# Four-layer spectral and convolution network on one core: complex sums on 128 partitions, inverse steps as two accumulating 64-row products

## The chip, the core and the metric

The kernel runs on one core of a Trainium2 chip. The core has TensorE (PE in the profile; its weight loads are listed apart as PEld), VectorE (DVE), ScalarE (ACT), GpSimd (POOL), and SyncE (SP), from whose queue nearly all DMAs are issued. PE writes its products to PSUM, which has eight banks of 2 KiB per partition; DVE and ACT read them there, POOL works on SBUF tiles alone. The metric is the device time of one execution in microseconds (us). Three timed runs of the kernel before took 786.98, 787.42 and 789.71 us; their median is 787.42.

## The reference

The input x is a sequence of 2048 rows with 512 channels in fp32. Four layers are applied in the order A, B, A, B, each on the layer norm of the running x and each added back to it:

```
def _A_ref(x, w_r, w_i):            # spectral layer
    X = rfft2(x) * (w_r + 1j * w_i)
    return irfft2(X, s=(S, D))

def _B_ref(u, ...):                 # long convolution per channel
    K = 2 * einsum("dn,dnl->dl", C, exp(A * dt * l)).real
    y = irfft(rfft(u, 2L) * rfft(K, 2L), 2L)[:, :L]
    return y + u * D_skip

x = x + _A_ref(_layernorm(x), ...);  x = x + _B_ref(_layernorm(x), ...)
x = x + _A_ref(_layernorm(x), ...);  x = x + _B_ref(_layernorm(x), ...)
```

What matters here is the middle of each layer: a spectrum is multiplied by complex weights (A) or by the spectrum of the convolution kernel (B), and is then transformed back.

## The kernel before, in words

All Fourier transforms are matrix products with constant matrices, split into small steps. The network runs through these stages:

- `layer_a` for the first A layer: `spread` (norm and the first step along the sequence), `middle` (16 groups q, each with `forward`, `weigh`, `back`, one group behind the other), `end` (`fold` and `rows_back`). Beside it runs `kernel_time`, which builds the convolution kernel K in the time domain and is the longest piece of work for DVE.
- `layer_b` for the first B layer: channels come in four blocks of 128. Per block there are the products along the rows (`forward_b.rows`), DVE transposes (`turn`), four `pair` products whose results `weigh` multiplies, the inverse products `back.units` and `back.rows`, and an add to x (line 1001). Between the four blocks stand the remaining three of the four blocks of `kernel_freq`, which take the spectrum of K by the same forward steps; what is left of `kernel_time` is filled in between.
- `layer_a` again, now without other work beside it, and `layer_b` again, whose K spectra are read back from DRAM (tile kk, line 956).

The order of the work on each engine is that of the lists of steps (`interleave`, and the lists in lines 1036 to 1064), within which the Tile framework orders instructions by priority and by its own model of time when the program is built. On the chip each engine takes its instructions in that fixed order.

The complex product in `layer_b.weigh` (lines 953 to 975). A `pair` fills one PSUM tile of 128 partitions by 512 for each of the two planes (real, imaginary). Its two partition halves are two halves h of the frequencies u, and each has 64 rows of spectrum for 32 channels. DVE multiplies each plane by the real and the imaginary part of the weights (line 962), which gives four tiles `m[c, pl]`. The sums are made by halves: for each h a subtraction of 64 partitions goes to partitions 0 to 63 of Y (the real part), and an addition to partitions 64 to 127 (the imaginary part). That is four sums of 64x512 per `weigh` (line 974), 16 per block. The strings `YB = 'vgggvggg'` and `YC = 'vgggvgggvgvgvgvv'` name the engine of each: v is DVE, g is POOL. YB, used twice over, puts 4 of a block's 16 sums on DVE; YC, used in the last block of each B layer, puts 7 there.

The inverse step. `units(j, d)` (line 977) treats 8 channels. For each it multiplies the 128 rows of Y (real over imaginary) by the constant MBT, in two products that go to the two partition halves of one PSUM bank; ACT copies the bank to V (line 987). `side_by_side` (line 308) only issues products after each other; two whose outputs lie in different partition halves use different column halves of PE's array and can run beside each other. Every fp32 product is two MATMUL and two LDWEIGHTS instructions in the trace. Before the first unit of a channel half, one product with the constant MIX replaces frequency 0 (line 982), with an ACT copy back to Y (line 983). `rows` (line 990) then makes the rows of the output.

In `layer_a`, `weigh(q)` (line 518) has the same form: four sums of 64x257 per q (lines 532, 533), with engines from YA and YA2, and one small sum for an edge column (line 534). `back(q)` (line 537) has four products of 128 rows, all into one PSUM bank, and two ACT copies (line 548).

PSUM pools. A `phase` line gives banks to tags: p1 holds forward products, p2 the pairs, p3 inverse products. In the first A layer p1, p2 and p3 share five banks. In the first half of the first B layer (`PM = '2,3,0'`, up to chain step 4) p1 and p3 share two; in its second half (`PB = [5, 3]`) they share five. From the second A layer on, p3 has three of its own.

## Time and profile before

| | |
|---|---|
| median of three timed runs | 787.42 us |
| profiled execution: span, first to last instruction | 781.1 us |
| what lies around the span (difference of the two) | 6.3 us |
| instructions | 18929 |
| ACT busy | 428.1 us (55%) |
| POOL busy | 404.9 us (52%) |
| DMA moved | 80.64 MB, mean 103 GB/s |
| mean granted TensorE clock | 0.934 |

The stages, read from the places of their lines in the trace (us from the start of the span): middle of the first A layer 78 to 156, its end 156 to 240, first B layer 285 to 540, middle of the second A layer 565 to 615, its end to 662, second B layer 662 to 781.

How to read it: a "lines" row gives line, engine, operation, tiles (out<-in), shape and count, then the busy time of the group (overlaps counted once), the mean duration of one in ns, the idle time of the engine just before them, and what ended it. "128*64" behind a matmul is the part of PE's array that it uses, rows by columns. PE's instructions overlap, so that a mean duration is far longer than the time per instruction. A "windows" row gives the stretch, its length, the busy time of each engine with its count of instructions, the granted clock, the DMA share and the rate. A "timeline" row gives start, time covered, engine, line, operation, and in brackets the idle time before it and its releaser.

### The profile page before, as it was taken

The page shows a single profiled execution, that of the slowest core. Times are in us where ns is not written, and L with a number is a line of the kernel's source. Part 1 is how long each engine was busy: PE and PEld are TensorE (multiplying, and loading weights), DVE is VectorE, ACT ScalarE, POOL GpSimd, SP SyncE. Part 2 cuts the span into 40 slices and gives each one's busy share as a digit, 9 for nine tenths or more (in the row PEclk, how much of TensorE's full clock was granted, in tenths as well). Part 3 has the DMA queues.
Part 4 walks back from the last instruction along what each step waited for, and adds up shares of the span by engine and source line. Part 5 has one row for each costly group of instructions (what it writes and reads, how often), then busy time and mean ns, then how long its engine had stood idle before and what let it go on. Part 6 is the DMA issues. An engine that isn't in the chain of part 4 may idle for free. (4 is left out here: it accounts for less than half of the span.)

```text
span 781.1 us, 18929 instructions
## 1 busy us (share of the span) xinstructions
PE 627.7 (80%) x7248; PEld 443.5 (57%) x7248; DVE 649.3 (83%) x1301; ACT 428.1 (55%) x919; POOL 404.9 (52%) x596
## 2 busy tenths in 40 slices
PE   3447888897867977998889887874899896989986
PEld 2336666665534543656365656654777663566766
DVE  7998748979998999769996997878578696889992
ACT  3433778854748765887568834323756336242312
POOL 3675876764825245721657266281055572475760
PEclk9998899999979997999989999997999999799998
DMA  8300552344546503452325539422133114234513
GB/s 311 128 0 1 129 138 56 110 75 151 114 167 184 137 9 64 124 145 82 51 68 117 192 55 257 141 95 69 55 82 83 28 28 136 70 95 120 154 29 83
DMA packets 144923, 80.64 MB, mean 103 GB/s; under 512 B 78561, under 2 KB 124513, under 8 KB 143937
## 3 DMA queue, kind: packets, MB, share of 16 engines
q1 hardware_dynamic: 144576, 78.90, 36.2%
q8 instruction: 58, 0.95, 0.5%
q0 software_dynamic: 256, 0.52, 0.4%
q14 instruction: 33, 0.26, 0.1%
HBM read 54.89 MB, written 25.03 MB: 102 GB/s over the span
## 5 line engine op out<-in xcount | busy, mean ns | idle before, releaser
L974 POOL TENSOR_TENSOR u<-wb,wb 64x512 f32<-64x512 f32 x90 | 129.2, 1436 | 85.2 <-DVE wb L962 75.9
L316 PE MATMUL p<-z,mb 128*64 128x512 f32 (+2 forms) x480 | 102.0, 535 | 8.3 <-DVE wb L962 5.4
L870 PE MATMUL pv<-qp 128*64 128x128 f32 x1024 | 78.9, 295 | 11.4 <-DVE qp L859 6.9
L859 DVE TENSOR_TENSOR qp<-qp,mag 128x1024 f32<-128x1024 f32 x64 | 83.8, 1317 | 1.0
L962 DVE TENSOR_TENSOR wb<-p,kk 128x512 f32<-128x512 f32 x128 | 80.6, 674 | 4.7 <-PE p L316 4.6
L870 PEld LDWEIGHTS pv<-qp 128*64 128x64 f32 x1024 | 62.0, 147 | 38.8 <-ACT stage L878 10.2
L648 ACT COPY z<-p 128x512 f32<-128x512 f32 x96 | 51.4, 597 | 58.1 <-PE p L316 43.7
L316 PE MATMUL p<-mb,u 128*64 128x64 f32 x2048 | 72.9, 235 | 10.6 <-DVE u L974 4.5
L316 PEld LDWEIGHTS p<-mb,u 128*64 128x64 f32 x2048 | 70.7, 150 | 18.7 <-issue 11.3
L857 DVE SCALAR_TENSOR_TENSOR qp<-qp,mag 128x256 f32<-128x256 f32 x128 | 64.8, 523 | 13.6 <-ACT qp L800 13.3
L654 DVE STREAM_TRANSPOSE z<-z 128x512 f32<-128x512 f32 x96 | 58.5, 673 | 18.0 <-ACT z L648 18.0
L527 DVE TENSOR_TENSOR w<-wt,p 128x514 f32<-128x514 f32 x64 | 42.6, 686 | 33.3 <-PE p L316 18.6
L1086 POOL TENSOR_SCALAR w<-w,norms 128x128 f32<-128x128 f32 x64 | 40.5, 647 | 51.9 <-DMA w<-h 28.3
L532 POOL TENSOR_TENSOR w<-w,w 64x257 f32<-64x257 f32 x48 | 40.1, 835 | 50.3 <-DVE w L527 46.2
L456 PE MATMUL p<-w,w 128*128 128x128 f32 x128 | 32.0, 429 | 40.8 <-DVE w L449 30.8
L987 ACT COPY u<-p 128x512 f32<-128x512 f32 x64 | 37.6, 590 | 43.8 <-PE p L316 43.8
L316 PEld LDWEIGHTS p<-z,mb 128*64 128x64 f32 x480 | 34.2, 140 | 37.0 <-issue 20.2
L456 PEld LDWEIGHTS p<-w,w 128*128 128x128 f32 x128 | 27.8, 318 | 44.7 <-issue 24.8
L800 ACT ACTIVATE kf<-pk 128x512 f32<-128x512 f32 x64 | 38.9, 608 | 24.1 <-PE pk L839 23.6
L316 PE MATMUL p<-t,w 64*64 64x128 f32 x1024 | 43.3, 290 | 5.8 <-issue 2.6
L974 DVE TENSOR_TENSOR u<-wb,wb 64x512 f32<-64x512 f32 x38 | 46.9, 1234 | 0.5
L800 ACT ACTIVATE qp<-kf,half 128x512 f32<-128x512 f32 x64 | 47.2, 737 | 0.1
(200 smaller groups left out, 1495.3 us busy)
## 6 DMA issues: line engine op xcount, KB each, us to landing
wt<-in_w SPq DMA_DIRECT2D x32, 257.0 KB
kf<-kk SPq DMA_DIRECT2D x32, 256.0 KB
kk<-kf SPq DMA_DIRECT2D x32, 256.0 KB
u<-in_x SPq DMA_DIRECT2D x16, 256.0 KB
hr<-in_x SPq DMA_DIRECT2D x16, 256.0 KB
kt<-stage SPq DMA_DIRECT2D x32, 128.0 KB
h<-hr SPq DMA_DIRECT2D x16, 256.0 KB
w<-kt SPq DMA_DIRECT2D x32, 128.0 KB
```

The lines of the kernel that those rows point to most:

```text
L316: last = self.nc.tensor.matmul(out, weights, data, start=not more, stop=True, skip_group_check=True).ins
L456: nc.tensor.matmul(p[:, b], xf[:, b], t, start=True, stop=True)
L527: nc.vector.tensor_mul(m[pl], W, px[:, None, :].to_broadcast([128, 2, 257]))
L648: nc.scalar.copy(tiles["z"][:, :, :, b, m:m + 2].rearrange("p u j m r -> p (u j) (m r)"), ps[b].rearrange("p u j m r -> p (u j) (m r)"))
L654: nc.vector.transpose(tiles["zt"][:, u:u + 8].rearrange("p u j d -> p (u j d)"), tiles["z"][:, u:u + 8].rearrange("p u j b m r -> p (u j b ...
L800: last["x"] = nc.scalar.activation(*a, **k).ins
L857: nc.vector.scalar_tensor_tensor(QP[:, c, 0], QP[:, c, 1, :, ::-1], -1.0 if c else 1.0, m[:, 0], op0=ALU.mult, op1=ALU.mult)
L859: nc.vector.tensor_mul(t, t, mag[:, None, 1:3, 256 * j:256 * j + 256].to_broadcast([128, 2, 2, 256]))
L870: nc.tensor.matmul(p[64 * t:64 * t + 64, g], QP[:, c, 2, d:d + 2].rearrange("p s a -> p (s a)"), QP[:, c, 0:2, d:d + 2].rearrange("p k s b ...
L962: nc.vector.tensor_mul(split(m[c, pl], "du", [32, 16]), by_channel(p), split(k[c], "du", [32, 16]))
L974: self.added = e[0].tensor_sub(y[0:64], v[0, 0], v[1, 1]), e[1].tensor_add(y[64:128], v[0, 1], v[1, 0])
L1086: (self.nc.gpsimd if XNE[k] == "g" else self.nc.vector).tensor_scalar(t[:, k], t[:, k], scale, bias, op0=ALU.mult, op1=ALU.add)
```

## The change

The 128 partitions that the complex product works on now hold two halves j of the channels, each with the same 64 rows of spectrum, where they held two halves of the frequencies. Real and imaginary parts of Y lie beside each other in one tile instead of one over the other.

- `pair`: the two halves of a PSUM tile are 16 channels each with all 32 frequencies of the step. The product for frequency 0 (i even) is now made for both halves.
- `weigh` in B: two sums of 128x512 instead of four of 64x512. YB puts both on POOL; YC puts those of the last `weigh` (i = 3) on DVE.
- `weigh` in A: two sums of 128x257 instead of four of 64x257, all on POOL.
- `units`: each product over 128 rows becomes two over 64 rows that add up in PSUM (r = 0, 1), for each channel half j (its own bank) and each half s of the output rows. So there are twice as many products, on quarters of the array (64 rows by 64 columns), and two banks are open at a time; a step now issues 32 products for 4 channels of both halves.
- `mix`: eight products of 64 rows by 16 columns in place of one of 128 by 32, two banks and two ACT copies in place of one.
- `back` in A: eight products of 64 rows in place of four of 128, two banks in place of one.
- Y and V become one tile of 32 KiB per partition in place of two of 16; U and the rows read at the start likewise. The constants grow (mb from 512 to 768 columns).

```diff
-YA = 'ggvg'
+YA = 'gg'
-YA2 = 'gvgv'
+YA2 = 'gg'
-YB = 'vgggvggg'
-YC = 'vgggvgggvgvgvgvv'
+YB = 'gggggggg'
+YC = 'ggggggvv'
...
-    return p.rearrange("p (u d) -> p d u", d=32)
+    return p.rearrange("p (u d) -> p d u", d=16)
...
             Y = self.sb("w", [2, 257])
-            for v in range(2):
-                hs = slice(64 * v, 64 * v + 64)
-                e = [nc.vector if c == "v" else nc.gpsimd for c in ya[2 * v:2 * v + 2]]
-                e[0].tensor_sub(Y[0:64, v], m[0][hs, 0], m[1][hs, 1])
-                e[1].tensor_add(Y[64:128, v], m[1][hs, 0], m[0][hs, 1])
+            e = [adders[c] for c in ya]
+            e[0].tensor_sub(Y[:, 0], m[0][:, 0], m[1][:, 1])
+            e[1].tensor_add(Y[:, 1], m[1][:, 0], m[0][:, 1])
...
-            p = self.ps("p3", [2, 2, 128])
+            p = [self.ps("p3", [2, 128]) for v in range(2)]
+            for oe in range(2):
+                for r in range(2):
+                    for v in range(2):
+                        hs = slice(64 * v, 64 * v + 64)
+                        nc.tensor.matmul(p[v][:, oe], Y[hs, r, 128 * oe:128 * oe + 128], k["ST"][hs, int(q + v > 0), r],
+                                         start=r == 0, stop=r == 1, skip_group_check=True)
             for v in range(2):
-                st = k["ST"][:, int(q + v > 0)]
-                for oe in range(2):
-                    nc.tensor.matmul(p[:, oe, v], Y[:, v, 128 * oe:128 * oe + 128], st, start=True, stop=True,
-                                     skip_group_check=True)
-            for oe in range(2):
-                nc.scalar.copy(U[oe].rearrange("p s n q (v c) -> p v (s n) q c", v=2)[:, :, :, q],
-                               p[:, oe].rearrange("p v (n c) -> p v n c", c=4))
+                nc.scalar.copy(U[2].rearrange("p o s n q (v c) -> p v o (s n) q c", v=2)[:, v, :, :, q],
+                               p[v].rearrange("p o (n c) -> p o n c", c=4))
...
-                products = []
-                for h in (1, 0):
-                    o = p[64 * h:64 * h + 64].rearrange("p (u d) -> p u d", d=32)
-                    u = 32 * (i % 2) + 16 * h
-                    c = 1 if u == 0 else 0
-                    z = tiles["zt"][:, :, i // 2]
-                    products += [(o[:, 0], MB[:, 0, pl], z[:, 0])] * c + [(o[:, c:], MB[:, 1, pl], z[:, u + c:u + 16])]
+                u = 32 * (i % 2)
+                c = 1 if u == 0 else 0
+                o = [p[64 * j:64 * j + 64].rearrange("p (u d) -> p u d", d=16) for j in range(2)]
+                z = [tiles["zt"][:, u:u + 32, j, 16 * (i // 2):16 * (i // 2) + 16] for j in range(2)]
+                products = [(o[j][:, 0], MB[:, 0, pl], z[j][:, 0]) for j in range(2 * c)]
+                products += [(o[j][:, c:], MB[:, 1, pl], z[j][:, c:]) for j in range(2)]
...
-            for h in range(2):
-                was = self.added
-                u = 32 * (i % 2) + 16 * h
-                y = Y[:, i // 2, :, u:u + 16]
-                v = {k: t[64 * h:64 * h + 64].rearrange("p (d u) -> p d u", d=32) for k, t in m.items()}
-                e = [nc.vector if c == "v" else eng for c in adders[4 * i + 2 * h:4 * i + 2 * h + 2]]
-                self.added = e[0].tensor_sub(y[0:64], v[0, 0], v[1, 1]), e[1].tensor_add(y[64:128], v[0, 1], v[1, 0])
+            d, u = 16 * (i // 2), 32 * (i % 2)
+            y = Y[:, :, d:d + 16, u:u + 32]
+            v = {k: split(t, "du", [16, 32]) for k, t in m.items()}
+            e = [nc.vector if c == "v" else eng for c in adders[2 * i:2 * i + 2]]
+            self.added = e[0].tensor_sub(y[:, 0], v[0, 0], v[1, 1]), e[1].tensor_add(y[:, 1], v[0, 1], v[1, 0])
...
-            def units(j, d):
-                if d == 0:
-
-                    pm = self.ps("p3", [32])
-                    with self.tc.issue_after(self.paired):
-                        nc.tensor.matmul(pm, MIX, Y[:, j, :, 0], start=True, stop=True)
-                    nc.scalar.copy(Y[:, j, :, 0], pm)
-                p = self.ps("p3", [64, 8])
-                self.side_by_side([(p[64 * r:64 * r + 64, :, i], Y[:, j, d + i], MBT[:, 64 * r:64 * r + 64])
-                                   for i in range(8) for r in range(2)])
-                nc.scalar.copy(V[:, :, j, :, d:d + 8].rearrange("p n q d -> p q n d"),
-                               p.rearrange("p (q n) d -> p q n d", q=2))
+            def mix(d):
+                pm = [self.ps("p3", [2, 16]) for j in range(2)]
+                with self.tc.issue_after(self.paired):
+                    self.side_by_side([(pm[j][hs, s], MIX[hs, r, 64 * s:64 * s + 64], Y[hs, r, d:d + 16, 0], *[r] * r)
+                                       for s in range(2) for r in range(2) for j, hs in enumerate(halves)])
+                for j, hs in enumerate(halves):
+                    nc.scalar.copy(Y[hs, :, d:d + 16, 0], pm[j][hs])
+
+            def units(d):
+                if d % 16 == 0:
+                    mix(d)
+                if d % 8 == 0:
+                    banks[:] = [self.ps("p3", [64, 8]) for j in range(2)]
+                self.side_by_side([(banks[j][64 * s:64 * s + 64, :, i % 8], Y[hs, r, i], MBT[hs, r, 64 * s:64 * s + 64], *[r] * r)
+                                   for i in range(d, d + 4) for r in range(2) for j, hs in enumerate(halves) for s in range(2)])
+                if d % 8 == 4:
+                    for j in range(2):
+                        nc.scalar.copy(V[:, :, j, :, d - 4:d + 4].rearrange("p n q d -> p q n d"),
+                                       banks[j].rearrange("p (q n) d -> p q n d", q=2))
```

62 lines of the change are left out of this document (33 added, 29 removed).

## The prediction, made before the changed kernel was run

> **What bounds the kernel now.** I read the page's first part, then the busy times by stage, then the groups, then the timeline of the second B layer and of the second A layer.
>
> ```profile
> PE 627.7 (80%) x7248; PEld 443.5 (57%) x7248; DVE 649.3 (83%) x1301; ACT 428.1 (55%) x919; POOL 404.9 (52%) x596
> ```
>
> Over the span no engine is full; the stages have to be looked at singly.
>
> ```profile
> core 0: us, PE busy (x) PEld busy (x) DVE busy (x) ACT busy (x) POOL busy (x), PEclk, DMA share, GB/s
> 78.00:156.00 78.00, 67.15 (x507) 49.94 (x506) 57.76 (x82) 63.57 (x138) 56.75 (x117) 0.91 0.42 108
> 285.00:540.00 255.00, 206.02 (x3007) 139.62 (x3006) 216.66 (x394) 147.32 (x285) 130.05 (x136) 0.92 0.43 112
> 662.00:781.00 119.00, 101.80 (x1870) 74.75 (x1870) 94.56 (x144) 34.86 (x67) 62.35 (x45) 0.93 0.31 90
> ...
> 565.00:615.00 50.00, 46.66 (x355) 35.14 (x355) 40.32 (x80) 29.34 (x87) 28.53 (x74) 1.00 0.29 75
> ```
>
> First B layer (285 to 540): DVE 216.7 and PE 206.0 of 255, nearly equal, DVE ahead. Second B layer (662 to 781): PE 101.8 of 119, DVE 94.6. Middle of the second A layer (565 to 615): PE 46.7 of 50. So DVE's relief counts in full only until PE is the more loaded, which comes soon. POOL (130 and 62 us) bounds nothing.
>
> In the second B layer PE's pauses are short. Three stand before the last row product of a block and are waits for DVE's add to x, which empties the PSUM bank:
>
> ```profile
> 710.76 1.09 PE L316 MATMUL p<-u,t 128*64 128x128 f32 x16 [1.50 <-DVE za L1001]
> ...
> 737.00 1.09 PE L316 MATMUL p<-u,t 128*64 128x128 f32 x16 [1.13 <-DVE za L1001]
> ...
> 758.75 1.09 PE L316 MATMUL p<-u,t 128*64 128x128 f32 x16 [2.08 <-DVE za L1001]
> ```
>
> Together 4.7 us: there DVE, late from its sums, holds PE up.
>
> **The sums, removed and added.**
>
> ```profile
> L974 POOL TENSOR_TENSOR u<-wb,wb 64x512 f32<-64x512 f32 x90 | 129.2, 1436 | 85.2 <-DVE wb L962 75.9 <-DVE wb L964 4.0
> L974 DVE TENSOR_TENSOR u<-wb,wb 64x512 f32<-64x512 f32 x38 | 46.9, 1234 | 0.5
> L532 POOL TENSOR_TENSOR w<-w,w 64x257 f32<-64x257 f32 x48 | 40.1, 835 | 50.3 <-DVE w L527 46.2 <-ACT kf L800 1.6 <-ACT w L511 0.7
> L533 POOL TENSOR_TENSOR w<-w,w 64x257 f32<-64x257 f32 x32 | 21.4, 669 | 2.3
> L533 DVE TENSOR_TENSOR w<-w,w 64x257 f32<-64x257 f32 x32 | 18.8, 587 | 1.1
> L532 DVE TENSOR_TENSOR w<-w,w 64x257 f32<-64x257 f32 x16 | 10.3, 644 | 1.5 <-DVE w L527 0.5
> L1062 POOL TENSOR_TENSOR t<-za 128x512 f32<-128x512 f32 x8 | 11.1, 1419 | 0.1
> ```
>
> A POOL sum over 128 partitions by 512 (line 1062) takes 1419 ns, one over 64 takes 1436: the partition count is free, so halving the number of sums halves the work. In B, 90 + 38 sums become 60 on POOL and 4 on DVE. POOL: 129.2 - 60 x 1.436 = 43.0 us less. In A, POOL 80 sums and DVE 48 become 64 on POOL: 61.5 - 64 x 0.75 (mean of its two rows) = 13.5 us less on POOL and 29.1 less on DVE.
>
> ```profile
> L974 DVE TENSOR_TENSOR u<-wb,wb x38: 671/1260/1799, 292.2 to 763.2; 64x512 f32<-64x512 f32 x38
> ...
> 285.00:540.00 255.00, 22.07 (x19) 66.85 (x45) 0.92 0.43 112
> ...
> 662.00:781.00 119.00, 24.83 (x19) 62.35 (x45) 0.93 0.31 90
> ```
>
> The second and third rows are line 974 alone, DVE then POOL. Per B layer DVE loses 22.1 and 24.8 us and gets two sums back, between 0.67 us (the minimum) and 1.80 (the maximum). I take 0.67, the nearest to an undisturbed one, so 1.3 per layer: net -20.7 and -23.5. The spread is POOL's doing: DVE operations with two SBUF inputs stretch while POOL works. An example:
>
> ```profile
> 313.77 6.23 POOL L974 TENSOR_TENSOR u<-wb,wb 64x512 f32<-64x512 f32 x3 [2.96 <-DVE wb L962]
> ...
> 315.69 1.48 DVE L857 SCALAR_TENSOR_TENSOR qp<-qp,mag 128x256 f32<-128x256 f32 x1
> ...
> 320.81 0.40 DVE L857 SCALAR_TENSOR_TENSOR qp<-qp,mag 128x256 f32<-128x256 f32 x1
> ```
>
> 1.48 us beside a POOL sum, 0.40 without. With fewer POOL sums this shrinks too; I count it at nothing, since DVE's net relief is already cut off by PE below.
>
> **What it is worth.** First B layer: the larger of the two loads falls from 216.7 (DVE) to 206.0 (PE; DVE would have 196.0), so -10.7. Bounds: 0 if PE's order sets the pace anyway; -20.7 / (216.7/255) = -24.4 if the stretch shrinks with DVE alone. Second B layer: PE is the larger load already, so only the three waits go, -4.7; bounds 0 and -11.5 (PE's idle 17.2 less the 5.7 between the last matmul, in a row below, and the end of the span). A layers: below.
>
> **The inverse units.** 2048 matmuls of 128x64 become 4096 of half the rows. What a matmul costs in a stream:
>
> ```profile
> 696.61 3.95 PE L316 MATMUL p<-mb,u 128*64 128x64 f32 x128
> ...
> 478.23 2.25 PE L316 MATMUL p<-t,w 64*64 64x128 f32 x72
> ...
> 771.66 3.71 PE L316 MATMUL p<-u,t 128*64 128x128 f32 x64 [0.73 <-ACT u L987]
> ```
>
> Per instruction 30.9 ns (64 columns streamed, two tiles of the array side by side), 31.3 (128 columns, four tiles), 58.0 (128 columns, two tiles). From the third to the second, four tiles instead of two halve the price at equal columns; from the third to the first, half the columns halve it. The new units have both, 64 columns on four tiles, which gives 15.5 ns, and 4096 x 15.5 = 63 us, as 2048 x 30.9 now. But no stream of the trace runs below 31 ns; the other end of the price is 31 ns each, +63 us of PE. I take 15.5: it follows two rows that differ in one thing each, and an end of 31 would mean that two different limits lie at the same number by chance.
>
> The TensorE page of the Trainium skill ("TensorE: Matmul & The Clock Gate", Wait — 56ns, not 53.3ns?) speaks against this: starts of matmuls are never closer than about 25 ns, however few columns. No row here is under it; estimated by that figure the 4096 cost 102 us in place of 63.
>
> **Banks and copies.** A group of 8 channels now fills two banks, both closed only with the group's last products.
>
> ```profile
> 768.22 0.59 ACT L987 COPY u<-p 128x512 f32<-128x512 f32 x1 [1.34 <-PE p L316]
> 769.16 0.59 ACT L987 COPY u<-p 128x512 f32<-128x512 f32 x1 [0.35 <-PE p L316]
> ```
>
> A copy takes 0.59 us and starts by the second row 0.35 us after the one before, when PE has filled the next bank; now it is hidden under that bank's products. Afterwards the two copies come together, the second free at 0.35 + 2 x 0.59 = 1.53 us after the last product, the first at 0.94. In the first half of the first B layer p3 and p1 have two banks in all, so the next group waits up to 1.53; elsewhere it has a spare bank and waits up to 0.94. 8 groups x 1.53 + 24 x 0.94 = 35 us if nothing else lay between; 0 if pairs, forward rows and the filled-in work always do. While a group waits, everything behind it in PE's fixed order waits too, pairs and forward rows among it, and behind these DVE's multiplications. But such work also stands ahead of nearly every group in the timeline, so I take a tenth, +3. The last group has nothing behind it: its second copy adds 0.6 to the end. `mix` has one more copy:
>
> ```profile
> L983 ACT COPY u<-p 128x32 f32<-128x32 f32 x16 | 3.6, 222 | 20.7 <-PE p L982 20.7
> ```
>
> 0.2 us each, on the path only at the last one, +0.2. The 96 additional small matmuls of `pair` are 3.0 us at 31 ns, half of that two at a time, a third of it in the second B layer: +0.5.
>
> The larger constants (256 more columns of 128 partitions in each of two loads, 131 KB) go through SP's queue before their stages:
>
> ```profile
> DMA packets 144923, 80.64 MB, mean 103 GB/s; under 512 B 78561, under 2 KB 124513, under 8 KB 143937
> ```
>
> At the mean rate 1.3 us each; the stages before cover them, and I count 0.
>
> The Trainium skill, "TensorEngine Tiling (Array Packing)", Gotcha 1: PSUM Pressure, says that row tiles must write to different banks. That is why two are open; by it the wait cannot be tuned away within one bank.
>
> **The A layers.** The middle of the second one is a PE loop of 3.0 us per q:
>
> ```profile
> 587.11 0.38 PE L499 MATMUL p<-ca,z 128*128 128x128 f32 x2
> ...
> 587.33 0.39 PE L500 MATMUL p<-ca,z 128*128 128x128 f32 x2
> ...
> 587.77 1.06 PE L545 MATMUL p<-ca,w 128*128 128x128 f32 x8
> ...
> 588.76 1.09 PE L316 MATMUL p<-w,ca 128*64 128x257 f32 x8
> ...
> 590.78 1.06 PE L545 MATMUL p<-ca,w 128*128 128x128 f32 x8
> ```
>
> From 587.11 to 587.33 two matmuls take 0.22; eight of the same kind should take 0.88, and from 587.77 to 588.76 they take 0.99 before other tiles are used. So a change of tiling costs 0.11. `back` now uses 64 rows by 128, another tiling than `forward`, with which it shared one: +0.11 x 16 = +1.8. Its 16 instructions run two at a time if row halves do as column halves do (the four-tile row has both), else +0.88 x 16 = +14 per A layer; I take the first. DVE's and POOL's relief is worth nothing here, PE covers it. In the first A layer PE has 11 us to spare of 78; its +1.8 and the shorter sums, which DVE waits for now and then, I set against each other, 0.
>
> **Sum.** -10.7 - 4.7 + 3 + 0.6 + 0.2 + 0.5 + 1.8 = -9.3. Span 781.1 - 9.3 = 771.8; with the 6.3 us by which the median of the three runs (787.42) exceeds the span, 778.1. I forecast 778.
>
> **Rivals.**
>
> Matmul rate (slower). Place: the units, in both B layers. If an instruction costs 31 ns whatever its columns, each layer gets +31.6 us of PE. Second B layer: 31.6 less the 11.5 that PE can absorb, +20. First: the load goes from 216.7 to 237.6, +21. With the rest (+6): about 834. It decides from the point where the extra E per layer eats the gain, (E - 11.5) + (E - 10.7) + 6.1 = 0, E = 8: 19.5 ns per matmul. At half of the extra, 23 ns, it gives 803. For it: no row under 31. Against it: the two halvings above.
>
> Banks. If half of the 35 us of waiting remains uncovered, +17 in place of +3: 792. For it: two banks in all in the first two blocks, and ACT has K's exponentials in its queue before the copies. Against it: three banks or more later.
>
> Full relief. If DVE sets the first B layer alone, and PE's pauses in the second go too: -24.4 - 11.5 + 6.1 = -29.8, 758. For it: DVE is delayed by POOL as well. Against it: PE at 81 to 86% in both.
>
> That the sums do not get cheaper on 128 partitions is excluded by line 1062; row halves of `back` one after the other give 778 + 14 to 28, and I give that little.
>
> **How the numbers follow.** Forecast (766 to 784) 0.44, full relief (750 to 766) 0.10, banks (784 to 797) 0.19, matmul rate (790 to 834) 0.23, row halves 0.04. The range 758 to 815 leaves out half of full relief and somewhat under half of the matmul rate, some 0.16. One half per cent of 787.4, 3.9 us, is about what a measurement of this kernel tells from no change. Faster, below 783.5: 0.43 + 0.10 + 0.02 = 0.55. Same: 0.01 + 0.11 + 0.01 = 0.13. Slower: 0.32.
>
> **What would show it.** POOL's L974 in 60 rows of 128x512 at some 1.4 us and DVE's in 4; the units as 4096 of 64*64, groups of 128 in about 2 us: right. The same groups in 4 us: the rate rival. PE or PEld idle before the units, released by ACT's copies, over 10 us: the banks. The middle of the second A layer at 3.1 us per q; at 4: row halves in turn. The three pauses before the last row products of the second B layer should be gone.
>
> What would make it wrong altogether is a new order: the framework arranges all engines anew, and DVE's K work beside POOL's sums may fall otherwise.

## The result, and the profile after it

The changed kernel takes 845.97 us (median of four runs, 843.26 to 849.8) beside 788.21 for the kernel before on the same chip. The two medians stand as 1.073 to 1; the ratio estimated from the single runs is 1.0755, 95% interval 1.0702 to 1.0808. The forecast was 778, range 758 to 815. Medians below are of all executions of a kernel, ratios of its fast ones alone (within 1.5% of its fastest), which leaves out two of four for e4 and for e9.

Of the profiled execution first the busy times, from the page, then four stages (middle of the first A layer, first B layer, middle of the second A layer, second B layer), which now lie at other places:

```profile
PE 673.4 (80%) x9872; PEld 463.3 (55%) x9872; DVE 572.8 (68%) x1219; ACT 431.5 (51%) x935; POOL 332.6 (39%) x550
```

```profile
core 0: us, PE busy (x) PEld busy (x) DVE busy (x) ACT busy (x) POOL busy (x), PEclk, DMA share, GB/s
78.00:156.00 78.00, 72.50 (x594) 51.88 (x591) 43.81 (x61) 56.53 (x127) 39.09 (x98) 0.91 0.41 107
285.00:575.00 290.00, 227.09 (x4307) 147.83 (x4303) 203.84 (x392) 164.46 (x320) 107.05 (x124) 0.90 0.38 100
597.00:663.00 66.00, 62.91 (x511) 46.70 (x509) 22.59 (x48) 33.01 (x95) 24.46 (x74) 0.95 0.21 57
707.00:846.00 139.00, 113.19 (x3040) 80.31 (x3040) 73.33 (x127) 36.90 (x79) 37.93 (x30) 0.91 0.27 78
```

DVE is relieved of 76 us and POOL of 72, and the span grew by 65. PE is busy 46 us longer. (The profiled execution of the kernel before was a quick one. In the other runs an execution takes 1.7 to 2.9 us more than its span, so its 781.1 us of span stand for some 783, below its four timed runs here; differences against its stages come out some 5 us too large in total.) The groups by shape of the changed kernel:

```profile
L316 PE MATMUL p<-mb,u 64*64 64x64 f32 x4096 | 80.8, 233 | 14.7 <-issue 9.6 <-ACT u L996 3.1 <-ACT u L985 1.7
L961 DVE TENSOR_TENSOR wb<-p,kk 128x512 f32<-128x512 f32 x128 | 80.5, 680 | 31.9 <-POOL u L972 25.2 <-PE p L316 3.5 <-ACT u L996 3.0
L972 POOL TENSOR_TENSOR u<-wb,wb 128x512 f32<-128x512 f32 x60 | 78.1, 1329 | 152.3 <-DVE wb L963 81.5 <-PE p L316 59.1 <-DVE wb L961 11.3
L530 POOL TENSOR_TENSOR w<-w,w 128x257 f32<-128x257 f32 x32 | 23.0, 718 | 63.9 <-DVE w L527 61.9 <-ACT stage L877 2.0
```

Two things can be read here. The sums cost a little less than was forecast (1329 ns in B for 1436, 718 in A for 750). And there are new waits at them: POOL's sums of a block wait 59.1 us for PE, which by the code still has to read the sums of the block before (the units come late), and DVE's multiplications wait 25.2 us for POOL, whose sums free the buffers that they write to. (Line 961 is line 962 of before, 972 its 974, 985 and 996 its 983 and 987, 1010 its 1001.)

### The profile page after: what moved, and what is told of

Same layout as the page of the kernel before. It is cut to its first block, busy times and chain, and to the rows that moved or that the text cites. A ratio compares the mean times of both kernels' runs of the same rounds, so it can differ in the third digit from the quotient of the medians.

```text
span 846.0 us, 24022 instructions
## 1 busy us (share of the span) xinstructions
PE 673.4 (80%) x9872; PEld 463.3 (55%) x9872; DVE 572.8 (68%) x1219; ACT 431.5 (51%) x935; POOL 332.6 (39%) x550
## 3 DMA queue, kind: packets, MB, share of 16 engines
q8 instruction: 78, 1.28, 0.6%
## 5 line engine op out<-in xcount | busy, mean ns | idle before, releaser
L972 POOL TENSOR_TENSOR u<-wb,wb 128x512 f32<-128x512 f32 x60 | 78.1, 1329 | 152.3 <-DVE wb L963 81.5
L316 PE MATMUL p<-z,mb 128*64 128x512 f32 (+2 forms) x576 | 111.3, 505 | 10.6 <-DVE z L654 7.8
L961 DVE TENSOR_TENSOR wb<-p,kk 128x512 f32<-128x512 f32 x128 | 80.5, 680 | 31.9 <-POOL u L972 25.2
L316 PE MATMUL p<-mb,u 64*64 64x64 f32 x4096 | 80.8, 233 | 14.7 <-issue 9.6
L316 PEld LDWEIGHTS p<-mb,u 64*64 64x64 f32 x4096 | 74.1, 146 | 30.7 <-issue 21.4
L856 DVE SCALAR_TENSOR_TENSOR qp<-qp,mag 128x256 f32<-128x256 f32 x128 | 58.8, 479 | 14.8 <-ACT qp L799 14.1
L996 ACT COPY u<-p 128x512 f32<-128x512 f32 x64 | 34.5, 591 | 63.4 <-PE p L316 63.4
L316 PEld LDWEIGHTS p<-z,mb 128*64 128x64 f32 x576 | 32.4, 146 | 52.9 <-issue 21.3
L545 PE MATMUL p<-ca,w 64*128 64x128 f32 x512 | 56.6, 310 | 5.1 <-POOL w L532 2.7
L837 DVE TENSOR_SCALAR kw<-pk 128x512 bf16<-128x512 f32 x64 | 43.5, 680 | 18.2 <-PE pk L835 17.9
L545 PEld LDWEIGHTS p<-ca,w 64*128 64x128 f32 x512 | 46.0, 204 | 17.3 <-issue 4.6
```

Source lines behind the costliest of these rows:

```text
L316: last = self.nc.tensor.matmul(out, weights, data, start=not more, stop=True, skip_group_check=True).ins
L545: nc.tensor.matmul(p[v][:, oe], Y[hs, r, 128 * oe:128 * oe + 128], k["ST"][hs, int(q + v > 0), r], start=r == 0, stop=r == 1, skip_group_c ...
L837: nc.vector.tensor_scalar(whole, p, MAGIC, -MAGIC, op0=ALU.add, op1=ALU.add)
L856: nc.vector.scalar_tensor_tensor(QP[:, c, 0], QP[:, c, 1, :, ::-1], -1.0 if c else 1.0, m[:, 0], op0=ALU.mult, op1=ALU.mult)
L961: nc.vector.tensor_mul(split(m[c, pl], "du", [16, 32]), by_channel(p), split(k[c], "du", [16, 32]))
L972: self.added = e[0].tensor_sub(y[:, 0], v[0, 0], v[1, 1]), e[1].tensor_add(y[:, 1], v[0, 1], v[1, 0])
```

## The experiments

For each run stands what was expected, word for word, and the median with its ratio to the kernel before, measured on the same chip. Stage lengths are read from the first and last instruction of a line in the trace: the end of the first B layer (its last row product), the middle of the second A layer (first product of `forward` to last of `back`) and the second B layer (first transposition to last row product). Each is of one profiled execution. The expectations of e1, e6 and e7 give the middle of the second A layer as 80 and 69 us; they count a longer stretch than the table's 66.1 and 54.5.

| run | median us | ratio, 95% | end of first B | middle of second A | second B |
|---|---|---|---|---|---|
| before (first chip) | 788.2 | | 532.1 | 54.5 | 109.4 |
| after | 846.0 | 1.070 to 1.081 | 567.6 | 66.1 | 128.1 |
| e2 A old, B new | 835.8 | 1.054 to 1.065 | 562.8 | 54.5 | 130.0 |
| e3 A new, B old | 821.5 | 1.036 to 1.053 | 560.3 | 64.3 | 108.4 |
| e5 half unit instructions | 809.3 | 1.023 to 1.035 | 543.9 | 65.9 | 114.5 |
| e10 the same, A old | 788.8 | 1.001 to 1.009 | 536.6 | 54.2 | 115.1 |
| e13 before, B sums on POOL | 813.7 | 1.030 to 1.039 | 559.5 | 55.3 | 110.2 |
| e14 before, A sums on POOL | 807.0 | 1.021 to 1.030 | 540.6 | 65.5 | 108.2 |
| e16 four banks | 832.4 | 1.053 to 1.064 | 572.3 | 56.1 | 122.6 |
| e18 back together | 848.2 | 1.073 to 1.087 | 567.4 | 65.9 | 127.9 |
| e19 together, four banks | 836.1 | 1.054 to 1.070 | 574.7 | 55.2 | 122.7 |

My first theory was that the costs of the parts came out as forecast and that all was lost to waits and order; its rivals were the price of the unit products and the banks.

### Which layers

One kernel takes the edits to `layer_a` back, the other those to `pair`, `kernel_freq` and `layer_b`. Both keep the one tile of 32 KiB in place of two of 16. Of the edits only the first lines are shown:

```diff
 e2, in layer_a as before:
-YA = 'gg'
+YA = 'ggvg'
...
 e3, in layer_b as before:
-YB = 'gggggggg'
+YB = 'vgggvggg'
...
```

> The A layers as before the change, the B layers and the kernel spectra as after it. Theory (part of the loss in the A layers: the DVE wait in the second one, and work on K pushed back in the first one by up to 19 us; the rest in the B layers through late units): 812 to 828. Rival 1 (all of the loss is in the B layers): 840 or more. Rival 2 (all of it comes from the A layers): under 792.

> The A layers as after the change, the B layers and the kernel spectra as before it. Theory: 788 plus the 11.6 us of the second A layer plus half to all of the 19 us by which K's work was late, 808 to 820. Rival 1 (all in the B layers): 785 to 792. Rival 2 (all in the A layers): 840 or more.

835.8 and 821.5. Either half alone loses, B 47.6 us and A 33.3; together they lose 57.8, not 81, because both make the first B layer late (by 30.7 and 28.2 us alone, by 35.5 together); that K's chain and the blocks wait for each other there is a reading of this, not shown. Both times lie above what was expected, by 7.8 and 1.5 us, and that of e2 is nearer to its rival (840 or more). The rivals that put all in one layer fall, since each half loses by itself.

### The units: the number of instructions

The first idea was order: mix and units as early in PE's order as they can be.

```diff
             def units(d):
+              with self.tc.high_priority(20000):
                 if d % 16 == 0:
```

> The changed kernel with the products of mix and units given high priority, so that they come in PE's order as early as their operands allow; in the built order the units of the second B layer's third block then stand ahead of 10 more products of the next pairs. Theory (units late in PE's order hold back POOL's next sums, and these DVE's multiplications): the second B layer shrinks by 8 to 18 us, the first by 5 or more, together 820 to 835. Rival (the two banks that a group fills set the pace, or the products themselves): 842 to 850.

848.7 (836.6 to 851.3; ratio 1.057 to 1.079). The wait of POOL's sums for PE fell from 59.1 to 13.9 us and that of DVE's multiplications for POOL from 25.2 to 3.9, but the time did not fall clear of the scatter: they are at most a part of the cost. So the products themselves:

```diff
-                self.side_by_side([(banks[j][64 * s:64 * s + 64, :, i % 8], Y[hs, r, i], MBT[hs, r, 64 * s:64 * s + 64], *[r] * r)
-                                   for i in range(d, d + 4) for r in range(2) for j, hs in enumerate(halves) for s in range(2)])
+                self.side_by_side([(banks[j][64 * s:64 * s + 64, :, i % 8], Y[:, j, i], MBT[:, j, 64 * s:64 * s + 64])
+                                   for i in range(d, d + 4) for j in range(2) for s in range(2)])
```

> The changed kernel, but its units issue 2048 products of 128 rows by 64 in place of 4096 accumulating ones of 64 rows, into the same two banks, from the same tile of sums and with the same copies; the products with the second part of each pair are left out, so what they compute is not the inverse step. By the burst rates of the traces (31 ns against 14.5) PE's time for them is the same. Theory 1 (PE is short of instructions: the pauses of 0.8 to 1.7 us inside the unit streams come beside 16 KB packets of the instruction queue, and 128 products of a stream need one packet): with half the instructions the pauses go, 6 to 10 us per B layer, 826 to 834. Theory 2 (units late in PE's order, two banks, waits of POOL and DVE): 841 to 851.

809.3, 36.7 us less, more than the theory of the instruction supply expected. (PE's time for the products is the same by their bursts, 2048 at 29.6 ns and 4096 at 14.7 from start to start.) The other direction, every unit of the changed kernel twice:

```diff
+for i in range(d, d + 4) for _ in range(2) for r in range(2) for j, hs in enumerate(halves) for s in range(2)
```

> The changed kernel with every unit product issued twice, which gives wrong sums and 4096 more matmul instructions in longer streams. Theory 1 (a sustained stream is held to the instruction supply, about 27 to 30 ns per matmul as the four last groups of the trace show): 955 to 970. Theory 2 (the stream keeps 14.5 to 16 ns, the pauses are waits for copies): 905 to 915.

935.8 (one execution): 89.8 us for 4096 more, 21.9 ns each, between the two expectations. What it shows is in PE's timeline of its second B layer:

```profile
909.61 5.66 PE L316 MATMUL p<-mb,u 64*64 64x64 f32 x253 [0.27 <-ACT u L985]
916.81 2.09 PE L316 MATMUL p<-mb,u 64*64 64x64 f32 x128 [1.54 <-issue]
920.56 2.09 PE L316 MATMUL p<-mb,u 64*64 64x64 f32 x128 [1.65 <-issue]
924.58 0.33 PE L316 MATMUL p<-mb,u 64*64 64x64 f32 x3 [1.93 <-issue]
```

At full granted clock a stream stops after every 128 products for some 1.6 us, with "issue", a wait for nothing that the profile shows. (The row of 253 has no stop; from 911 to 913 us its granted clock is 0.50 and the products come more slowly.) From 916.81 to 920.56 is 3.75 us: 29.3 ns per product, whatever the burst. Counted in the trace, weight loads included, the stops of over 0.4 us in the second B layer follow each other after 256 instructions or a multiple of 256, to within one: all 22 intervals of this run, and all 6 of the changed kernel. What runs out is found in the third part of the pages, the row of the instruction queue (packets, MB, share), of the changed kernel and of this run:

```profile
q8 instruction: 78, 1.28, 0.6%
```

```profile
q8 instruction: 110, 1.80, 0.8%
```

The run has 2 x 4096 products and weight loads more and 32 packets more: one packet for 256 instructions, which is a burst of 128 products. And PE's waits of this kind (total, times, longest), in the kernel before, the changed one, e5 and e8:

```profile
PE p L316 <- issue: 6.5, 9, 1.8
```

```profile
PE p L316 <- issue: 17.8, 16, 4.6
```

```profile
PE p L316 <- issue: 3.6, 4, 1.8
```

```profile
PE p L316 <- issue: 58.5, 46, 4.1
```

The last block of the second B layer, where little else runs, shows it in the changed kernel and then in e5 (PE's timeline):

```profile
820.55 2.28 PE L316 MATMUL p<-mb,u 64*64 64x64 f32 x132 [0.32 <-ACT u L985]
823.48 0.45 PE L316 MATMUL p<-mb,u 64*64 64x64 f32 x12 [0.64 <-ACT u L996]
825.39 2.62 PE L316 MATMUL p<-mb,u 64*64 64x64 f32 x110 [1.46 <-issue]
...
829.95 3.59 PE L316 MATMUL p<-mb,u 64*64 64x64 f32 x132 [0.17 <-ACT u L985]
834.19 2.08 PE L316 MATMUL p<-mb,u 64*64 64x64 f32 x124 [0.66 <-ACT u L996]
```

```profile
786.97 2.20 PE L316 MATMUL p<-mb,u 128*64 128x64 f32 x68 [0.55 <-ACT u L985]
789.67 1.97 PE L316 MATMUL p<-mb,u 128*64 128x64 f32 x60 [0.50 <-ACT u L996]
...
793.40 2.20 PE L316 MATMUL p<-mb,u 128*64 128x64 f32 x68 [0.51 <-ACT u L985]
796.11 1.97 PE L316 MATMUL p<-mb,u 128*64 128x64 f32 x60 [0.51 <-ACT u L996]
```

15.7 us (820.55 to 836.27) against 11.1, with the same banks and copies and waits of 0.2 to 0.7 us for them in both. The group at 829.95 takes 3.59 us without a stop, for another reason: by the busy times of a stretch in it the granted clock (the figure 0.50) is halved there, and from start to start a product takes 26.7 ns instead of 14.6. That is some 1.4 of the 4.6 us by which this block is longer. By the table the four blocks of the second B layer lose 13.6 us to e5's, and the first B layer loses 23.7.

```profile
830.60:832.70 2.10, 2.10 (x90) 2.10 (x85) 0.00 (x0) 0.00 (x0) 0.00 (x0) 0.50 0.00 0
```

A run was to give each instruction half the work: e5's products, each cut into two of 32 columns.

```diff
-for i in range(d, d + 4) for j in range(2) for s in range(2)
+for i in range(d, d + 4) for j in range(2) for h in range(2) for s in range(2)
```

> The kernel of the half units (128-row products, second part left out) with every one of them cut into two of 32 columns: 4096 unit instructions again, in the same order of the steps, with the same copies and waits, and with half the work in each. Theory (the number of PE instructions costs, through their supply, not the work in them): back to 838 to 848. Rival (the number of instructions is free, it was the order of the framework or the accumulating pairs): 806 to 814.

885.6 (871.4 to 888.2; ratio 1.104 to 1.131), outside both. The groups of that kernel tell why:

```profile
L316 PE MATMUL p<-mb,u 128*64 128x32 f32 x4096 | 139.0, 231 | 5.6 <-ACT u L985 2.9 <-issue 1.6 <-ACT u L996 1.1
```

From start to start a product of 32 columns on two tiles takes 29 ns like one of 64, so the work was not halved, and at 29 ns the supply just keeps up (1.6 us of "issue"). The run says nothing for or against the supply. That the number of instructions costs is shown by e5 and e8. That the supply is the reason for the stops rests on their distance of 256 instructions and the packets of that size. The waits under "issue" account for 14.2 of e5's 36.7 us; how the rest divides between what follows from late units and the other order that the framework builds for half as many products was not separated.

The edits of e2 and e5 together:

> A layers as before, B layers as changed but with the half units (inverse step not computed in full). Theory: the relief of the sums is real and shows when neither the A layers nor the number of unit instructions hide it; from the run with new A layers and half units, 809, less the 33 us that the new A layers alone cost, 772 to 784. Rival (the B layers gain nothing from fewer sums): 786 to 795.

788.8, ratio 1.001 to 1.009: the rival. With old A layers and half the unit instructions the sums' relief (DVE 193.6 us busy between 285 and 540 in place of 216.7) brings nothing; the first B layer ends 4.5 us later than before and the second is 5.7 longer.

### What DVE's load is worth

```diff
-YB = 'vgggvggg'
-YC = 'vgggvgggvgvgvgvv'
+YB = 'gggggggg'
+YC = 'gggggggggggggggg'
```

> The kernel before with one thing different: all sums of the B layers on POOL (128 of 64x512 there, none on DVE), the layout and PE's work as before. DVE loses 46.9 us of sums, POOL gets some 38 more. Theory (PE and K's chain set the pace of the B layers, not DVE's load): no gain, 786 to 800. Rival (DVE bounds the first B layer, as the forecast had it): 770 to 782.

813.7, above both ranges. In the old layout DVE is relieved of all sums of B and the first B layer ends 27 us later; the second is unchanged. The waits of PE from 285 to 560, in the kernel before and in this one:

```profile
PE p L316 <- POOL u L974: 1.9, 1, 1.9
```

```profile
PE p L316 <- POOL u L974: 19.8, 2, 14.8
```

And those of POOL in the same stretch, in the same order:

```profile
POOL e L821 <- ACT mag L800: 14.1, 4, 11.6
```

```profile
POOL e L821 <- ACT mag L800: 48.1, 7, 25.0
POOL w L1086 <- PE pk L836: 38.1, 3, 18.8
```

POOL takes its instructions in order. Sums stand behind K's operations (line 821) and the norm's (line 1086), which wait for ACT and PE, and PE then waits for the sums. By these waits the one sum in four on DVE kept the chain off POOL's queue. Whether fewer sums moved would have cost less was not run.

The same for the A layers of the kernel before (`YA = 'gggg'`, `YA2 = 'gggg'`):

> The kernel before with all sums of both A layers on POOL (four of 64x257 per q), the layout as before. Theory 1 (the sums' move to POOL makes K late in the first A layer and holds up the second): K's fourth group begins after 270 us in place of 256, the middle of the second A layer takes over 60 us in place of 54.5, 800 to 825. Theory 2 (the accumulating pairs, the second bank or the one tile of 32 KiB do it): 785 to 795.

807.0: 11 us in the second A layer, whose multiplications wait for POOL, and 8.5 until the end of the first B layer. K's fourth group (of eight, by its first product `pv`) begins at 256 us in the kernel before, at 262 there, at 285 in the changed kernel: the engine of the sums explains the second A layer in the old layout, and little of K's lateness.

And in the changed kernel (`YA = 'gv'` for `'gg'`):

> The changed kernel with one of the two sums per q of the first A layer on DVE. Theory 1 (all sums on POOL make K late): K's fourth group begins before 275 us in place of 285 and the first B layer ends 8 to 20 us earlier, 826 to 838. Theory 2 (the order that the framework builds, whichever engine sums): within 5 us of 846.

857.3 (1.085 to 1.093), outside both: K's fourth group at 288. The sums' engine is not what makes K late. Two other runs bear on it. In e2, which has the A layers as before but the one tile of 32 KiB, the group begins at 260.5, so that tile isn't it either. And in e5 it begins at 285 as in the changed kernel, yet the first B layer ends 23.7 us earlier: K's lateness alone does not set that end.

### The loop of the second A layer

The middle takes 66.1 us in place of 54.5, 4.1 us per q.

First the edge sum, which DVE makes after POOL's sums (`YE2 = 'g'` for `'v'`):

> The changed kernel with one letter different: in the second A layer the small edge sum goes to POOL, behind the two sums that it needs, and no longer to DVE. Theory (a wait that the move of all sums to POOL made): the middle of the second A layer shrinks from 80 us to the 69 us it had before, and the time falls by 10 to 12 us, to about 835. Rival (the row halves of the inverse product and their tiling cost the time): the middle stays at 79 to 81 us and the time at 846.

848.0 (1.070 to 1.080), the rival's time, middle 64.2: the edge sum is not it. POOL's timeline in the changed kernel:

```profile
623.53 0.19 POOL L515 COPY wt<-ends 128x4 f32<-128x4 f32 x1 [2.51 <-DMA wt<-in_w]
623.67 0.64 POOL L530 TENSOR_TENSOR w<-w,w 128x257 f32<-128x257 f32 x1
624.27 0.64 POOL L531 TENSOR_TENSOR w<-w,w 128x257 f32<-128x257 f32 x1
...
627.72 0.19 POOL L515 COPY wt<-ends 128x4 f32<-128x4 f32 x1 [2.50 <-DMA wt<-in_w]
```

POOL stands still for 2.5 us per q before a small copy that waits for the weights' DMA, with both sums behind it. And SP's waits (603 to 650 us):

```profile
SPq L513 <- POOL w L504: 34.3, 10, 3.8
```

The load of the next weights waits for POOL (line 504 is a small memset right behind the sums in POOL's order). So: sums, load, copy, sums, 4.15 us. Three runs cut it at different places, one with a sum on DVE (`YA2 = 'gv'`), one with the copy on ACT (`WE2 = 'a'`), one with buffers of their own for the weights (`wx=(2056, 3)` in the phase of x, and W taken from it); a fourth halves the products of `back`:

> The changed kernel with one of the two sums per q of the second A layer on DVE. Theory (the loop of the second A layer's middle is: POOL's copy of the weights' edge waits for the DMA of the weights, both sums stand behind it in POOL's queue, the sums free the buffer into which the next weights are loaded; 2.6 us of DMA, 0.2 of copy and two times 0.6 of sums give the 4.1 us per q): with one sum off POOL the loop loses at least 0.6 us per q, the middle falls from 80 to 69 or 71 us and the time to 834 to 838. Rival (row halves and changes of tiling on PE): 844 to 848.

> The changed kernel with the copy of the weights' edge in the second A layer on ACT instead of POOL; both sums stay on POOL. Theory (the sums stand behind a copy that waits for a DMA): the sums start when DVE has multiplied, the middle falls to 69 to 72 us and the time to 834 to 838. Rival 1 (two sums one after the other on POOL are too long, whatever stands ahead): the middle stays at 78 to 81 and the time at 844 to 848. Rival 2: ACT takes the wait over and its copies come late, so the middle gains nothing.

> The changed kernel with three buffers of its own for the weights of the second A layer, which share seven buffers with the products and sums there. Theory (the DMA of the weights waits for POOL's sums to free a buffer, and so 2.6 us of DMA stand in the loop): SP issues the loads early, the loop falls from 4.1 to at most 3.3 us per q and the time by 10 to 13 us, to 833 to 836. Rival (POOL's sums one after the other are the loop): 843 to 848.

```diff
-                for r in range(2):
-                    for v in range(2):
-                        hs = slice(64 * v, 64 * v + 64)
-                        nc.tensor.matmul(p[v][:, oe], Y[hs, r, 128 * oe:128 * oe + 128], k["ST"][hs, int(q + v > 0), r],
...
+                for v in range(2):
+                    nc.tensor.matmul(p[v][:, oe], Y[:, v, 128 * oe:128 * oe + 128], k["ST"][:, int(q + v > 0), v],
...
```

> The changed kernel with the inverse products of both A layers as four of 128 rows in place of eight accumulating ones of 64 rows (the second part is left out, so they do not compute the inverse step), still into two banks; the sums stay on POOL. Theory (K's work in the first A layer is late because twice as many inverse products stand ahead of it in PE's order): K's first pv product stands back at 130 us in place of 138, the first half of the B layer follows, 815 to 832. Rival (the sums on POOL make K late): 842 to 848.

Middle and median: e6 59.6 and 842.4 (1.064 to 1.074), e7 61.1 and 850.6 (1.073 to 1.085), e11 61.5 and 847.8 (1.072 to 1.087), e12 51.9 and 838.0 (1.061 to 1.076). The middle gets shorter in all, most in e12, and the medians follow badly: e6 and e12 lie between their two ranges, e7 above both, e11 at its rival's. Part of that is scatter: e7's PE and DVE take the same instructions in the same order as the changed kernel's, and in its profiled execution the first B layer, which it does not touch, ends 9.6 us later. The middle itself scatters less, 64 to 67.4 us in e3, e4, e5, e8, e9 and e17, which leave it as it is. What e11 and then e12 show is in SP's waits in the same stretch; the load waits for POOL no more in either:

```profile
SPq L513 <- DVE w L527: 43.6, 13, 3.9
```

```profile
SPq L513 <- DVE w L532: 18.0, 11, 2.0
SPq L513 <- PE p L543: 13.6, 12, 2.8
```

Yet e11's loop still takes about 4 us per q, so there is something beside POOL and the load. e12 has both sums on POOL and the shared buffers, and takes 3.0 us per q with half the products of `back`: so the sums on POOL close a loop only together with the doubled products and their order. PE's timeline, changed kernel, then e16:

```profile
624.23 0.49 PE L497 MATMUL p<-ca,z 128*128 128x132 f32 x2
...
625.10 0.49 PE L545 MATMUL p<-ca,w 64*128 64x128 f32 x2
625.51 0.49 PE L501 MATMUL p<-ca,z 128*128 128x128 f32 x2
625.93 1.16 PE L545 MATMUL p<-ca,w 64*128 64x128 f32 x14
627.02 1.09 PE L316 MATMUL p<-w,ca 128*64 128x257 f32 x8
```

```profile
617.44 1.16 PE L545 MATMUL p<-ca,w 64*128 64x128 f32 x16
618.53 0.65 PE L316 MATMUL p<-w,ca 128*64 128x257 f32 x4
619.12 0.49 PE L497 MATMUL p<-ca,z 128*128 128x132 f32 x2
...
619.89 0.39 PE L501 MATMUL p<-ca,z 128*128 128x128 f32 x2
620.21 0.66 PE L316 MATMUL p<-w,ca 128*64 128x257 f32 x4
```

The framework put two of `back`'s 16 instructions ahead of `forward`'s last product. By their starts in the trace, 86 of the 128 row-half pairs run together in the second A layer; the others run one after the other, 0.11 us apart or more. `back` (line 545) then keeps PE busy for 28.3 us there, against 18.8 before. In e16 all 16 instructions stand together, all 128 pairs run together and `back` takes 19.8. That run changes only the banks:

```diff
-                outer.enter_context(net.phase("pc", P, p1=(2048, 2), p2=(2048, 3), p3=(2048, 3)))
+                outer.enter_context(net.phase("pc", P, p1=(2048, 2), p2=(2048, 2), p3=(2048, 4)))
```

> The changed kernel with four PSUM banks for inverse products and two for the pairs from the second A layer on, where it has three and three. Theory (a unit group needs two banks, three let only one group be open, so that PE waits for ACT's copies, 7.3 us in the second B layer, and the framework puts units behind other work): the second B layer falls from 128 us by 5 to 10, 836 to 841. Rival (instruction supply alone): 844 to 848.

832.4, below the expected range: 13.6 us less than the changed kernel; in the profile the second A layer is 10.0 us shorter and the second B layer 5.5. Last, the eight products of `back` kept together, alone and with four banks:

```diff
...
+            self.side_by_side([(p[v][:, oe], Y[64 * v:64 * v + 64, r, 128 * oe:128 * oe + 128], k["ST"][64 * v:64 * v + 64, int(q + v > 0), r], *[r] * r)
+                               for oe in range(2) for r in range(2) for v in range(2)])
```

> The changed kernel with the eight inverse products of each q of the A layers bound to one another in PE's order, halves alternating, nothing else changed. Theory (the framework splits the group and sets products of the same row half behind each other, so that 42 of 128 pairs run one after the other, 7 to 8 us of PE per A layer): all 128 pairs start together, the middle of the second A layer falls from 66 to 55 to 58 us, K in the first is up to 7 us earlier, 830 to 838. Rival (the sums on POOL or two banks of three hold the loop): the middle stays at 62 us or more, 841 or more.

> The same, and four PSUM banks for inverse products and two for pairs from the second A layer on. Theory: the second A layer as in the run before, the second B layer 122 to 124 us in place of 128, together 824 to 833; what then stays above the 788 of before is K's lateness and the instruction supply of the units. Rival (both edits mend the same wait): as the run with four banks alone, 830 to 836.

848.2 (1.073 to 1.087) and 836.1 (1.054 to 1.070): the first as its rival had it, the second above the theory's range and at the upper end of the rival's, that both edits mend the same wait. In e18 108 pairs run together and the middle stays at 65.9. Its loads still wait for POOL, 31.1 us between 603 and 650, and two instructions of `back` still stand ahead of `forward`'s last product, so PE's order is mended only in part (`back` is busy for 25.0 us). My reading is that two loops of nearly the same length lie there, POOL with the load and PE's order; e11 breaks the one and gains 4.6 us of the middle, e18 mends part of the other and gains nothing. Four banks change the order, and with it both: in e16 the loads are released by PE and DVE, and a q takes 3.35 us. No run beats the kernel before.

## Why the prediction was wrong

**What it is worth** failed. It took the larger of DVE's and PE's load as the length of the first B layer (-10.7) and three waits for the second (-4.7). The three waits did go (one of 0.55 us is left) and DVE's load moved as worked out (193.6 us in e10, forecast 196.0), but e10 and e13 show that DVE's load did not set either stage. Two of the 19 sums that DVE had in the first B layer (22.1 us) are left in e10 and none in e13, and the layer ends 4.5 and 27 us later. DVE at 85% with K's chain through PE, ACT, POOL and DVE is, as I read it, a chain of waits and not a full engine. The lower bound, 0, was nearest. The sentence that POOL bounds nothing went by its busy time alone; e13 and e14 show that moving sums to it costs 27 and 20 us. The 6.3 us that the sum puts around the span are 1.7 to 2.9 in the other runs; the rest is that the profiled execution was quicker than the median.

**The inverse units** failed in their sustained price. The burst is near the forecast (14.6 ns from start to start; 16.3 as the forecast counted, the time covered divided by the count, for 15.5), but the step multiplied a burst by 4096. By e5 the second half of the instructions costs 36.7 us, by e10 and e2 47.0, which is 9.0 and 11.5 ns for each of the 4096: a mean of 24 or 26 ns with the burst's 14.6, late units and a new order included, beyond the 19.5 that the rival on the matmul rate named as its turning point. That rival had the sign and the place, and its 834 came nearest; its mechanism (a floor for one instruction) was not the one found. The reading that half the columns halve the price held from 128 to 64 columns, but not below: e9 shows 29 ns at 32 columns on two tiles, as at 64.

The Trainium skill, "TensorE: Matmul & The Clock Gate", section "Wait — 56ns, not 53.3ns?", says that starts are never closer than about 25 ns. That does not hold here (14.6 on four tiles), though 29.3 sustained comes near what it would have given. Another page of the Trainium skill, "Runtime: NRT & Kernel Launch", section "Instruction fetch mechanics", says that instructions come in blocks of 16 KiB, 256 instructions, and that the fetch is mostly hidden; the first agrees with 1.28 MB in 78 packets, the second does not where a product takes less than 29 ns.

**The A layers**: 1.8 for the second was 11.6. The rival of row halves in turn (+14 per layer, little chance) came about for a third of the pairs (42 of 128), through the order, and `back` keeps PE busy 9.5 us longer; the loop of POOL and the load was not seen at all. The prediction looked at PE's 3.0 us alone and took the relief of DVE and POOL as worth nothing, not asking what stands behind a waiting instruction in POOL's queue. For the first A layer 0 was taken; K's fourth group is late by 29 us. The runs exclude as the main reason the sums' engine (e17), the one tile (e2) and the number of inverse products (e12: K's first product is back at 129.7 us, as expected, but the fourth group begins at 281). That it is the order built anew is argued, not shown; the second bank that `back` takes of the five shared ones was not taken back alone and is a rival. This stays open.

**Banks and copies**: +3 was too little. Four banks give back 13.6 us, though by the stages through the order in the A layer more than through waits for copies (PE waits 9.1 us for line 996 in all, 1.5 for line 987 before). **The sums' own cost** (POOL 1.33 us over 128 partitions), **pair**, and the **constants** came out as forecast.

The closing warning, that the framework arranges all engines anew, was right and had no number: e14 and e13 change only the engine of some sums and move the whole by 20 and 27 us.

## What to carry to other kernels

Before halving an engine's load, ask whether the stage is a full engine or a chain: a sum on a second engine may be there to keep the chain out of a queue in which instructions wait for DMAs. When a product is split into more and shorter ones, count instructions as well as array time, and price a long stream by a long stream, not by a burst. If an experiment that removes a wait gains nothing, look for a second loop of the same length before giving up the first.

## What the runs showed of the hardware that was not expected

- PE streams 64x64 products on four tiles at 14.6 ns each from start to start, but in e8, at full granted clock, stops for some 1.6 us after each 128 of a long stream; sustained 3.75 us per 128, 29.3 ns. The stops of the second B layer lie 256 instructions or a multiple of it apart.
- On two tiles the price from start to start is 29 ns at 32 columns (e9) and at 64 (29.4 in the kernel before, 29.6 in e5).
- Two products on different row halves can start 7 ns apart: 86 of 128 pairs in the order of the changed kernel, 108 with the halves bound to alternate (e18), 128 with four banks (e16). The others start at least 0.1 us apart.
- The mean granted clock fell from 0.934 to 0.889, about a third of it in a stretch where it costs nothing: from 30 to 60 us the clock is 0.50 in the changed kernel, PE's busy time is that of before at 1.00, and DVE is full. The same stretch has 1.00 in e3 and e16 and 0.50 in e13, so it follows neither layout.

```profile
30.00:60.00 30.00, 14.84 (x60) 12.83 (x58) 30.00 (x72) 12.45 (x28) 23.86 (x39) 0.50 0.00 0
```
